# A chunked recurrence fused with a multiplicative FFN on one core: one cumulative sum instead of two from the ninth unit on, and the last output tile stored in two halves

## The chip, the core and the metric

The kernel runs on one core of one Trainium2 chip. The time is device microseconds of one launch. Lower is better.

A core has a tensor engine (PE, with its weight loads shown apart as PEld), a vector engine (DVE), a scalar engine (ACT), a general engine (POOL) and a sync engine (SP) that here only issues DMAs. Each engine works through its own queue in the order in which the program lists its instructions.

## The reference, cut to what matters

Attention: four batches, eight heads, 768 tokens, head size 48. The state of a head decays by `w` per channel and takes in an outer product per token:

```
for t in range(S):
    cur = einsum('bhd,bhe->bhde', u * k[t], v[t])
    y[:, :, t] = einsum('bhd,bhde->bhe', r[t], state + cur)
    state = w[t][..., None] * state + einsum('bhd,bhe->bhde', k[t], v[t])
```

Its result, 3072 tokens by 384 channels, goes through an FFN: `a = x @ w1`, `b = x @ w2` (384 to 1024), `h = a * b @ w3` (1024 to 1024), `out = h @ w_out` (1024 to 384). All inputs and the output are float32.

## The kernel before, in words

**Units.** The tokens are cut into 24 units of 128 tokens (4 batches of 6 units, all eight heads together: a tile of 128 partitions by 384). The step-by-step recurrence becomes matrix work per unit (`att(n)`): with the running sum of log w, k is multiplied by exp(-sum) and r by exp(sum), and a masked product of the two gives what a token takes from earlier tokens of its unit. A state per head pair carries the rest from unit to unit. The steps of a unit `n`, with the engine that does each:

- `ld_w`, `ld_k`, `ld_r`, `ld_v`: four loads of 192 KB each, issued by SP. k and r share a tile `kr_in`; there are eight of each input tile.
- `ln` (ACT): `lw` = log w, in bfloat16.
- `cs0`, `cs1` (PE): two matmuls of 384 columns, with constant triangular matrices `LTn_incl` (minus the sum up to and with the token) and `LT_strict` (the sum up to the token before). Each takes one of five PSUM banks (tiles `g`) which the attention steps share.
- `ex0`, `ex1` (ACT): exp in place in those banks.
- `krt0`, `krt1` (DVE): k and r times the two exponentials, to bfloat16 (`krt`). `krt1` needs `ex1` and the load of r.
- `tr` (PE, eight transposes) and `trs` (the copy out of PSUM) for units 0 to 12; from unit 13 on (`kr_dma`) one DMA transpose issued by SP takes the place of both.
- `vb` (v to bfloat16), `kv` (PE: the unit's contribution to the state, and the unit's whole decay), `pc` (ACT: exp of that decay), `ts`, `st` (DVE: the state), `sb` (its bfloat16 copy).
- `m` (PE: k by r, two banks), `mb0`, `mb1` (DVE: the mask), `y` (PE), `yb` (DVE), `yt` (PE transposes) and `xt` (copy): the FFN's input `xT`.
- `uk1`, `uk2` (POOL: u·k·r, in two multiplications, on tile `uk`), `ds` (DVE: a sum per head) and `yd` (POOL): the token's own term. `uk2` is the last step that reads r as loaded, beside `krt1`.

**FFN.** Nine blocks of 1, 2, 3, 3, ... units. For a block `j`, eight pairs `a`, `b` (three matmuls each), a copy of `a` (`as`, ACT) and a product (`ab`, DVE); then for each of its units `o` (eight matmuls of 384 columns), a copy out of PSUM (`os`) and a store (`st`). The products w3 @ w_out are made once (`wt`, `wtc`, `wm`, `wc`: tiles w3T, wm, w) as soon as those weights are there, so that the FFN needs no h. FFN tiles have three PSUM banks of their own.

**Order.** Nothing is reordered at run time. `Plan` (lines 53 to 208) has a list of steps, each with an engine, an assumed length, what it needs, what buffers or banks it takes and frees, and a rank. It goes through time, starts on each engine the step that can start first (rank breaks ties), and so fixes the order of every engine's queue. `TUNE["nudge"]` shifts single ranks; `TUNE["other"]` lists the steps that go to their second engine (for `trs`, `wtc`: the other of ACT and DVE; `xt`, `os`, `wc`: DVE for ACT; `vb`, `sb`: ACT for POOL; `st`: the ACT queue for SP's). `att` (lines 397 to 585) adds the steps of a unit, `ffn_out` (lines 624 to 646) the output steps, and units are added at a set distance ahead of the FFN. The five big weight loads are issued by POOL, each behind a step named in `TUNE["triggers"]`. Early gaps of PE are filled with matmuls on zeros (`busy`) that compute nothing. Since all instructions go through the helper at line 222, the profile shows that line for all of them; groups are told apart by their tiles.

Of the kernel before, what the change touches and what calls it, by code (L numbers as in the profile page):

```python
# [7 lines left out]
F32 = mybir.dt.float32  # L8
# [10 lines left out]
    kr_dma=13,  # L19
    pair=0,  # L20
    ahead=3, fill=48, cold=9,
    other=[
        "trs0", "trs1", "trs2", "sb2", "sb3", "xt3", "vb4", "xt4", "wc4", "vb6", "sb6", "wtc6", "wc7", "sb7", "vb8",
        "sb8", "st1.0", "xt9", "xt12", "st2.2", "xt13", "vb14", "sb14", "os3.0", "st3.0", "os3.1", "st3.1", "xt16",
        "xt17", "vb18", "vb20", "sb20", "xt20", "os5.0", "st5.1", "xt22", "xt23", "os7.0", "st7.1", "os7.2",
        "st7.2", "st8.1", "st8.2"],
    nudge={
        "ld_w0": -2, "ld_r0": -2, "ld_r6": -27, "ld_w8": -9, "ld_k8": -8, "ld_r8": -34, "ld_v8": -8, "ld_k9": 3,
        "ld_v9": 3, "ld_w10": -1, "ld_w13": 8.5, "ld_k13": 13.5, "ld_k14": -5, "ld_v14": 2, "ld_w15": 7, "ld_k15":
        7, "ld_v15": 7, "ld_w16": 12, "ld_k16": 11, "ld_v16": 12, "ld_w18": -2, "ld_k20": 33, "ld_k21": 30,  # L30
        "ld_v21": 43, "ld_w22": 101, "ld_k22": 33, "ld_r22": 849, "ld_v22": 196, "ld_w23": 139, "ld_k23": 514,
        "ld_v23": 535, "vb1": 75, "yd1": 126, "uk12": 78, "ds2": -49, "tr3": -115, "kv3": -196, "sb3": 175, "yt3":
        210, "cs0.4": -191, "krt1.4": -100, "uk14": 58, "wt1": -93, "wt2": 67, "wt3": 71, "ex0.5": 139, "krt0.5":
        -208, "cs1.5": -36, "ex1.5": -60, "krt1.5": -66, "m5": -29, "ds5": 626, "yt5": 229, "wt4": -42, "wm5": -165,
        "cs0.6": -253, "cs1.6": -84, "tr6": -130, "kv6": -205, "sb6": -168, "m6": 104, "y6": -120, "yb6": 211,
        "wt6": 84, "wtc6": 318, "wt7": 46, "ln7": 59, "cs0.7": 66, "kv7": -219, "ts7": 240, "sb7": -317, "uk17":
        149, "yb7": -88, "o0.0": -59, "a1.0": -276, "ex1.8": -234, "vb8": 49, "kv8": -283, "pc8": -151, "st8": -301,
        "mb0.8": -84, "a1.5": 142, "a1.6": -143, "a1.7": 37, "cs1.9": -90, "krt1.9": 31, "tr9": 31, "pc9": -141,
        "st9": 48, "ds9": 131, "yd9": 147, "b2.0": 416, "krt0.10": 110, "cs1.10": -75, "krt1.10": 402, "vb10": -358,
        "m10": -330, "ds10": 198, "y10": -242, "yt10": 176, "cs1.11": -53, "ex1.11": 492, "krt1.11": 48, "tr11": 26,  # L40
        "vb11": 154, "m11": -426, "mb1.11": -113, "ln12": -56, "cs0.12": 23, "krt0.12": 467, "cs1.12": 35, "ex1.12":
        -181, "tr12": -252, "uk112": 111, "yb12": 314, "a3.0": -100, "a3.2": 46, "b3.2": 183, "cs0.13": -426,
        "krt0.13": -254, "cs1.13": -20, "krt1.13": 33, "kv13": -107, "pc13": -221, "mb1.13": 183, "uk113": 242,
        "ds13": 23, "y13": 40, "xt13": 121, "b3.6": 155, "cs0.14": -79, "cs1.14": -104, "ds14": 313, "vb15": 51,
        "ds15": 111, "y15": -97, "a4.2": 87, "krt0.16": 84, "a4.4": 742, "ln17": -366, "cs1.17": 186, "krt1.17":
        288, "uk117": 572, "ds17": 29, "o4.2": 318, "cs0.18": -437, "krt0.18": 374, "ds18": -91, "y18": 72, "yb18":
        87, "yt18": 1247, "b5.1": 166, "a5.2": 446, "ts19": -150, "a5.6": -448, "b5.7": -40, "o5.0": 409, "o5.2":
        107, "krt1.21": 75, "cs1.22": -204, "y22": 132, "cs0.23": -34, "m23": 94, "o6.1": 17, "o6.2": 537, "a7.1":
        83, "a7.4": 106, "o7.0": 192, "a8.0": -392, "o8.2": -59},
# [177 lines left out]
def kernel(  # L227
# [88 lines left out]
    NS = 3  # L316
# [11 lines left out]
    plan.buffers(w_in=NIN, kr_in=NIN, v_in=NIN, lw=NS, krt=NS, v_bf=3, uk=2, ds=2, yd=3,  # L328
# [28 lines left out]
    def bank(step):  # L357
        return banks(step)[0]
# [37 lines left out]
    def att(n):  # L396
        b, c = divmod(n, NC)
        last = c == NC - 1
        kr_dma = n >= TUNE["kr_dma"]
# [5 lines left out]
        def cs(j):  # L405
            t = T["cs", n, j] = bank(f"cs{j}.{n}")
            pe.matmul(t[:, 0:DM], lhsT=(LTn_incl, LT_strict)[j], rhs=T["lw", n][:, :, 0:D], start=True, stop=True)

        def ex(j):
            t = T["cs", n, j][:, 0:DM]  # L410
            act.activation(t, t, Act.Exp)

# [41 lines left out]
        def kv():  # L454
            t = T["kv", n] = bank(f"kv{n}")[:, 0:HP * (D + 1)].rearrange("d (p e) -> d p e", p=HP)
            for p in range(HP):
                for q in range(2):
                    pe.matmul(t[q * DP:(q + 1) * DP, p, 0:D], lhsT=T["krt", n][:, 0, 2 * p + q, :],
                              rhs=T["vb", n][:, 2 * p + q, :], start=True, stop=True)
            for p in range(HP):  # L460
                pe.matmul(t[:, p, D:D + 1],
                          lhsT=T["lw", n][:, 2 * p:2 * p + 2, :].rearrange("t h d -> t (h d)"),
                          rhs=ones_c, start=True, stop=True)

        def pc():
            t = T["kv", n][:, :, D:D + 1]
            act.activation(t, t, Act.Exp)

        def ts():
            t = T["ts", n] = work.tile([C, HP, D], F32, tag="ts", name="ts_")  # L470
            if c == 0:
                dve.tensor_copy(t, T["kv", n][:, :, 0:D])
            else:
                dve.tensor_add(t, T["st", n - 1], T["kv", n][:, :, 0:D])

        def st():
            t = T["st", n] = work.tile([C, HP, D], F32, tag="st", name="st_")
            dve.tensor_mul(t, T["ts", n], T["kv", n][:, :, D:D + 1].to_broadcast([C, HP, D]))
# [65 lines left out]
        A(f"ln{n}", "ACT", 0.5, ln, needs=[f"ld_w{n}"], take=["lw"], free=[f"ld_w{n}"])  # L544
        for i in range(2):
            A(f"cs{i}.{n}", "PE", 0.165, lambda i=i: cs(i), needs=[f"ln{n}"], bank=1, lag=0.2,
              free=[f"ln{n}"] if i else [])
            A(f"ex{i}.{n}", "ACT", 0.46, lambda i=i: ex(i), needs=[f"cs{i}.{n}"])
            A(f"krt{i}.{n}", "DVE", 0.52, lambda i=i: krt(i),
              needs=[f"ex{i}.{n}", f"ld_k{n}", f"ld_r{n}"][:3 if i else 2] + [f"krt0.{n}"] * i, take=["krt"] * (1 - i),  # L550
              free=[f"cs{i}.{n}", f"ld_k{n}"])
        if not kr_dma:
            A(f"tr{n}", "PE", 0.54, tr, needs=[f"krt1.{n}"], bank=1, lag=0.2, free=[f"krt0.{n}"])
            A(f"trs{n}", "ACT", 0.98, trs, needs=[f"tr{n}"], take=["trs"], free=[f"tr{n}"], alt=("DVE", 0.68))
        else:
            A(f"trs{n}", "SP", 1.8, trs, needs=[f"krt1.{n}"], take=["trs"], free=[f"krt0.{n}"], rows=1500, rank=-3)
        A(f"vb{n}", "POOL", 0.52, vb, needs=[f"ld_v{n}"], take=["v_bf"], free=[f"ld_v{n}"], alt=("ACT", 0.49))
        if not last:
            A(f"kv{n}", "PE", 0.36, kv, needs=[f"krt0.{n}", f"vb{n}"], bank=1, lag=0.2, free=[f"krt0.{n}", f"ln{n}"])
            A(f"pc{n}", "ACT", 0.18, pc, needs=[f"kv{n}"])  # L560
            old = [f"st{n - 1}"] if c else []
            A(f"ts{n}", "DVE", 0.32, ts, needs=[f"kv{n}"] + old, take=["ts"], free=old)
            A(f"st{n}", "DVE", 0.32, st, needs=[f"ts{n}", f"pc{n}"], take=["st"], free=[f"ts{n}", f"kv{n}"])
            A(f"sb{n}", "POOL", 0.7, sb, needs=[f"st{n}"], take=["sb"], free=[f"st{n}"], alt=("ACT", 0.5))
        if pair:
            A(f"m{n}", "PE", 0.33, m, needs=[f"trs{n}"], take=["m"], lag=0.2)
            A(f"mb0.{n}", "DVE", 1.19, lambda: mb(0), needs=[f"m{n}"], take=["mbf"], free=[f"m{n}"])
        else:
            A(f"m{n}", "PE", 0.33, m, needs=[f"trs{n}"], bank=2, lag=0.2)
            for q in range(2):  # L570
                A(f"mb{q}.{n}", "DVE", 0.65, lambda q=q: mb(q), needs=[f"m{n}"] + [f"mb0.{n}"] * q,
                  take=["mbf"] * (1 - q), free=[f"m{n}:{q}"])
        A(f"uk1{n}", "POOL", 1.03, uk1, needs=[f"ld_k{n}", "uc"], take=["uk"])
        A(f"uk2{n}", "POOL", 1.03, uk2, needs=[f"uk1{n}", f"ld_r{n}"], free=[f"ld_k{n}"])
        A(f"ds{n}", "DVE", 0.52, ds, needs=[f"uk2{n}"], take=["ds"], free=[f"uk1{n}"])
# [48 lines left out]
    def ffn_out(j, t_):  # L624
# [7 lines left out]

        def os():
            t = T["os", j, t_] = work.tile([P, DM], F32, tag="o_sb", name="o_sb", bufs=3)
            copy_on(f"os{j}.{t_}", t, T["o", j, t_])

        def st():
# [4 lines left out]
          take=["f"], lag=0.2, free=[f"ab{j}.0"] if t_ == hi - lo - 1 else [])  # L642
        A(f"os{j}.{t_}", "ACT", 0.45, os, needs=[f"o{j}.{t_}"], take=["o_sb"], free=[f"o{j}.{t_}"], rank=EV,
# [108 lines left out]
```

## Time and profile before

| | |
|---|---|
| median of 9 runs | 181.47 us (180.4 to 184.51) |
| the profiled execution | 180.4 us |
| its span, first to last instruction | 178.7 us |
| PE, DVE, ACT, POOL busy | 169.6, 138.8, 101.8, 90.0 us |
| granted clock of PE | 0.997 |
| bytes read and written | 27.8 and 4.7 MB |

How to read it: the span is what the trace covers; the 1.7 us beside it are the launch's. "Busy" adds up the time in which an engine had an instruction under way. A matmul's duration in the trace runs from its start to its modelled end, and the next one starts before that; so what a matmul costs a PE with no gaps is the distance from one start to the next. Rows of groups read: engine, operation, out<-in, shape, count, then busy us and mean ns of one, then idle time of the engine before them and who ended it.

### The profile page before, as it was taken

The page shows a single profiled execution, that of the slowest core. Times are in us where ns is not written, and L with a number is a line of the kernel's source. Part 1 is how long each engine was busy: PE and PEld are TensorE (multiplying, and loading weights), DVE is VectorE, ACT ScalarE, POOL GpSimd, SP SyncE. Part 2 cuts the span into 40 slices and gives each one's busy share as a digit, 9 for nine tenths or more (in the row PEclk, how much of TensorE's full clock was granted, in tenths as well). Part 3 has the DMA queues.
Part 4 walks back from the last instruction along what each step waited for, and adds up shares of the span by engine and source line. Part 5 has one row for each costly group of instructions (what it writes and reads, how often), then busy time and mean ns, then how long its engine had stood idle before and what let it go on. Part 6 is the DMA issues. An engine that isn't in the chain of part 4 may idle for free.

```text
span 178.7 us, 4690 instructions
## 1 busy us (share of the span) xinstructions
PE 169.6 (95%) x1738; PEld 106.6 (60%) x1738; DVE 138.8 (78%) x296; ACT 101.8 (57%) x235; POOL 90.0 (50%) x133
## 2 busy tenths in 40 slices
PE   7989878999999999999999999999999999999992
PEld 2445356777676756667665665655656656566560
DVE  7587735735998998998999899898989988864520
ACT  4333137425697799896787485574656753424421
POOL 4399460207288658489851577951569265100000
PEclk9999999999999999999999999999999999999998
DMA  6999999998999999999999999999999998103013
GB/s 117 192 190 212 200 220 191 194 207 169 193 195 178 241 193 207 189 168 220 233 202 177 186 260 182 188 224 161 206 211 165 229 172 189 22 25 111 0 68 108
DMA packets 117832, 31.23 MB, mean 175 GB/s; under 512 B 111921, under 2 KB 116018, under 8 KB 117810
## 3 DMA queue, kind: packets, MB, share of 16 engines
q1 hardware_dynamic: 113616, 24.72, 82.8%
q0 software_dynamic: 2896, 4.46, 13.6%
q10 hardware_dynamic: 1298, 1.77, 3.2%
q8 instruction: 13, 0.21, 0.5%
q14 instruction: 9, 0.07, 0.2%
HBM read 27.79 MB, written 4.72 MB: 182 GB/s over the span
## 4 chain that ended last, share of the span: by engine, by line
PE 78%; ACT 2%; issue 1%; DVE 0%; ACTq 0%
PE g L222 19%; PE a L222 17%; PE b L222 17%; PE o_ps L222 17%; PE wm L222 6%; PE wt L222 2%; ACT o_sb L222 1%; DVE w3T L222 0%; ACT sbd L222 0%; ACT g L222 0%; ACT xT L222 0%; ACT lw L222 0%; ACTq L222 0%; ACT trs L222 0%
## 5 line engine op out<-in xcount | busy, mean ns | idle before, releaser
L222 PEld LDWEIGHTS <-w_bf 128*128 128x128 bf16 x496 | 41.8, 97 | 23.0 <-issue 2.0
L222 ACT COPY a_sb<-a 128x384 f32<-128x384 f32 (+2 forms) x72 | 31.9, 444 | 29.8 <-PE a L222 27.7
L222 DVE TENSOR_TENSOR abT<-a_sb,b 128x384 bf16<-128x384 f32 (+2 forms) x72 | 36.5, 507 | 10.7 <-ACT a_sb L222 5.5
L222 PE MATMUL b<-xT,w_bf 128*128 128x384 bf16 (+2 forms) x216 | 43.1, 308 | 1.2 <-DMA w_bf<-in_moe_w_dram 1.1
L222 PE MATMUL a<-xT,w_bf 128*128 128x384 bf16 (+2 forms) x216 | 43.1, 308 | 0.5 <-ACT xT L222 0.5
L222 PE MATMUL o_ps<-w,abT 128*128 128x384 bf16 x192 | 34.3, 326 | 0.0
L222 DVE TENSOR_TENSOR mbf<-g,mask 128x512 bf16<-128x512 f32 x48 | 31.8, 685 | 1.7 <-PE g L222 1.6
L222 POOL TENSOR_TENSOR uk<-kr_in,u_bc 128x384 f32<-128x384 f32 x24 | 23.9, 997 | 13.0 <-DMA kr_in<-in_k_dram 12.1
L222 ACT ACTIVATE g<-g 128x384 f32<-128x384 f32 (+1 forms) x68 | 24.8, 385 | 8.4 <-PE g L222 6.4
L222 DVE TENSOR_TENSOR krt<-kr_in,g 128x384 bf16<-128x384 f32 x48 | 25.6, 549 | 5.1 <-ACT g L222 3.6
L222 POOL TENSOR_TENSOR uk<-uk,kr_in 128x384 f32<-128x384 f32 x24 | 24.0, 999 | 8.8 <-DMA kr_in<-in_r_dram 7.4
L222 POOL TENSOR_TENSOR yd<-v_bf,ds 128x384 bf16<-128x384 bf16 x24 | 19.8, 829 | 16.0 <-DVE ds L222 11.6
L222 PEld LDWEIGHTS <-abT 128*128 128x128 bf16 x192 | 18.2, 97 | 11.0
L222 ACT ACTIVATE lw<-w_in 128x384 bf16<-128x384 f32 x24 | 12.6, 524 | 7.5 <-DMA w_in<-in_w_dram 5.4
L222 POOL CAST v_bf<-v_in 128x384 bf16<-128x384 f32 x18 | 9.0, 505 | 14.8 <-DMA v_in<-in_v_dram 10.4
L222 ACT COPY o_sb<-o_ps 128x384 f32<-128x384 f32 x19 | 9.1, 479 | 12.0 <-PE o_ps L222 11.6
L222 PEld LDWEIGHTS <-trs 48*128 48x128 bf16 (+1 forms) x272 | 10.7, 95 | 8.6 <-issue 2.5
L222 PEld LDWEIGHTS <-krt 128*64 128x64 bf16 (+1 forms) x264 | 10.6, 105 | 8.0 <-issue 3.2
L222 DVE TENSOR_TENSOR y_bf<-g,yd 128x384 bf16<-128x384 f32 x24 | 13.3, 553 | 1.5 <-PE g L222 0.9
L222 DVE TENSOR_REDUCE ds<-uk 128x8 f32<-128x384 f32 x24 | 13.1, 544 | 0.0
L222 PE MATMUL idle<-busy 128*128 128x512 bf16 (+8 forms) x38 | 10.8, 399 | 1.3 <-DVE busy L222 1.3
L222 PE MATMUL wm<-wo_bf,w3T 128*128 128x384 bf16 x64 | 11.4, 327 | 0.0
(114 smaller groups left out, 188.1 us busy)
## 6 DMA issues: line engine op xcount, KB each, us to landing
w_in<-in_w_dram SPq DMA_DIRECT2D x24, 192.0 KB, 4.6
kr_in<-in_k_dram SPq DMA_DIRECT2D x24, 192.0 KB, 4.5
kr_in<-in_r_dram SPq DMA_DIRECT2D x24, 192.0 KB, 4.5
v_in<-in_v_dram SPq DMA_DIRECT2D x24, 192.0 KB, 4.4
out_dram<-o_sb SPq DMA_DIRECT2D x15, 192.0 KB, 3.4
w_bf<-in_moe_w_dram POOLq DMA_DIRECT2D x2, 1024.0 KB, 13.4
out_dram<-o_sb ACTq DMA_DIRECT2D x9, 192.0 KB, 3.4
w_bf<-in_moe_w_dram POOLq DMA_DIRECT2D x2, 768.0 KB, 9.0
```

What stands on the lines that cost most here:

```text
L222: return self.tc.keep_in_program_order(f(*a, **k))
```

## The change

Two things in the code, and a new list of choices.

From unit 8 on (`one`), there is one cumulative sum. `cs0` alone is computed, as before minus the sum up to and with the token. `ex0` writes exp of it into a second bank; `ex1` writes exp of its negative in place. That second one is one token too far for r, so r is multiplied by exp(-log w): `wi` (ACT) makes that from `lw`, and `rw` (POOL) multiplies it into the loaded r in place, after `uk2` has read it. `krt1` needs `rw` where it needed the load of r. The matmul with `LT_strict` is gone for these 16 units.

The output tile of the last unit is copied out in two halves of 192 columns, the first by ACT and the second by DVE, and each half has its own store, from the ACT queue and from SP's.

`TUNE["other"]` and `TUNE["nudge"]` are new throughout, and three assumed lengths of PE steps in the plan are others (`tr` 0.45 for 0.54, `kv` 0.44 for 0.36, `m` 0.42 for 0.33). A variant `wide` of `kv` and `ts` is written but switched off (99). The triggers, the blocks and `kr_dma` stay.

```diff
+    wide=99,
+    one=8,
     other=[
-        "trs0", "trs1", "trs2", "sb2", "sb3", "xt3", "vb4", "xt4", "wc4", "vb6", "sb6", "wtc6", "wc7", "sb7", "vb8",
-        "sb8", "st1.0", "xt9", "xt12", "st2.2", "xt13", "vb14", "sb14", "os3.0", "st3.0", "os3.1", "st3.1", "xt16",
-        "xt17", "vb18", "vb20", "sb20", "xt20", "os5.0", "st5.1", "xt22", "xt23", "os7.0", "st7.1", "os7.2",
-        "st7.2", "st8.1", "st8.2"],
+        "xt0", "sb2", "sb3", "wtc0", "xt4", "wc1", "wc4", "st0.0", "xt8", "xt9", "os1.1", "sb10", "xt10", "vb11",
+        "st2.0", "st2.2", "vb14", "sb14", "os3.0", "st3.0", "st3.1", "st3.2", "sb15", "sb16", "xt16", "vb17",
+        "os4.1", "st4.1", "st4.2", "vb18", "sb18", "xt19", "vb20", "sb20", "os5.2", "st5.2", "xt23"],
     nudge={
-        "ld_w0": -2, "ld_r0": -2, "ld_r6": -27, "ld_w8": -9, "ld_k8": -8, "ld_r8": -34, "ld_v8": -8, "ld_k9": 3,
...
-        7, "ld_v15": 7, "ld_w16": 12, "ld_k16": 11, "ld_v16": 12, "ld_w18": -2, "ld_k20": 33, "ld_k21": 30,
-        "ld_v21": 43, "ld_w22": 101, "ld_k22": 33, "ld_r22": 849, "ld_v22": 196, "ld_w23": 139, "ld_k23": 514,
-        "ld_v23": 535, "vb1": 75, "yd1": 126, "uk12": 78, "ds2": -49, "tr3": -115, "kv3": -196, "sb3": 175, "yt3":
...
+        "ld_w5": -1, "ld_k7": -1.5, "ld_w10": -2, "ld_v11": -1, "ld_k13": -2, "ld_w15": 2.5, "ld_r15": 1, "ld_w16":
+        -3, "ld_v16": -10, "ld_w19": -2, "ld_w20": -2, "ld_r20": -2, "ld_w22": 49, "ld_k22": 178, "ld_v22": 212,
+        "ld_v23": 534, "mb0.0": -31, "mb1.0": -16, "ds0": -89, "yd0": -119, "krt0.1": -90, "krt1.1": -74, "ts0.1":
...
+        def ex_one(j):
+            if j == 0:
+                T["cs", n, 1] = T["cs", n, 0]
+                T["cs", n, 0] = bank(f"ex0.{n}")
+            act.activation(T["cs", n, j][:, 0:DM], T["cs", n, 1][:, 0:DM], Act.Exp, scale=(1.0, -1.0)[j])
+
+        def wi():
+            t = T["wi", n] = work.tile([C, H, D], F32, tag="wi", name="wi")
+            act.activation(t, T["lw", n][:, :, 0:D], Act.Exp, scale=-1.0)
+
+        def rw():
+            t = T["kr_in", n][:, 1]
+            pool.tensor_mul(t, t, T["wi", n])
...
+        if one:
+            A(f"cs0.{n}", "PE", 0.165, lambda: cs(0), needs=[f"ln{n}"], bank=1, lag=0.2, free=[f"ln{n}"])
+            A(f"ex0.{n}", "ACT", 0.47, lambda: ex_one(0), needs=[f"cs0.{n}"], bank=1)
+            A(f"ex1.{n}", "ACT", 0.47, lambda: ex_one(1), needs=[f"ex0.{n}"])
+            A(f"wi{n}", "ACT", 0.5, wi, needs=[f"ln{n}"], take=["wi"], free=[f"ln{n}"])
         for i in range(2):
-            A(f"cs{i}.{n}", "PE", 0.165, lambda i=i: cs(i), needs=[f"ln{n}"], bank=1, lag=0.2,
-              free=[f"ln{n}"] if i else [])
-            A(f"ex{i}.{n}", "ACT", 0.46, lambda i=i: ex(i), needs=[f"cs{i}.{n}"])
+            if not one:
+                A(f"cs{i}.{n}", "PE", 0.165, lambda i=i: cs(i), needs=[f"ln{n}"], bank=1, lag=0.2,
+                  free=[f"ln{n}"] if i else [])
+                A(f"ex{i}.{n}", "ACT", 0.46, lambda i=i: ex(i), needs=[f"cs{i}.{n}"])
             A(f"krt{i}.{n}", "DVE", 0.52, lambda i=i: krt(i),
-              needs=[f"ex{i}.{n}", f"ld_k{n}", f"ld_r{n}"][:3 if i else 2] + [f"krt0.{n}"] * i, take=["krt"] * (1 - i),
-              free=[f"cs{i}.{n}", f"ld_k{n}"])
+              needs=[f"ex{i}.{n}", f"ld_k{n}", f"rw{n}" if one else f"ld_r{n}"][:3 if i else 2] + [f"krt0.{n}"] * i,
+              take=["krt"] * (1 - i),
+              free=[f"{'ex0' if i == 0 else 'cs0'}.{n}" if one else f"cs{i}.{n}", f"ld_k{n}"])
...
+        if one:
+            A(f"rw{n}", "POOL", 1.0, rw, needs=[f"wi{n}", f"uk2{n}"], free=[f"wi{n}"])
...
+        def os_half(i):
+            t = T["os", j, t_, i] = work.tile([P, DM // 2], F32, tag=f"o_h{i}", name="o_h", bufs=1)
+            copy_on(f"os{j}.{t_}.{i}", t, T["o", j, t_][:, i * DM // 2:(i + 1) * DM // 2])
...
+        if lo + t_ == NU - 1:
+            for i, (e, length, q) in enumerate((("ACT", 0.27, "ACT"), ("DVE", 0.32, "SP"))):
+                A(f"os{j}.{t_}.{i}", e, length, lambda i=i: os_half(i), needs=[f"o{j}.{t_}"], free=[f"o{j}.{t_}"], rank=EV)
+                A(f"st{j}.{t_}.{i}", q, 0.4, lambda i=i: st_half(i), needs=[f"os{j}.{t_}.{i}"], rows=225, rank=-1)
+            return
```

## The prediction, made before the changed kernel was run

> **What bounds the kernel now.** First the page's busy line and its slices.
>
> ```profile
> PE 169.6 (95%) x1738; PEld 106.6 (60%) x1738; DVE 138.8 (78%) x296; ACT 101.8 (57%) x235; POOL 90.0 (50%) x133
> ...
> PE   7989878999999999999999999999999999999992
> ...
> DVE  7587735735998998998999899898989988864520
> ...
> PEclk9999999999999999999999999999999999999998
> DMA  6999999998999999999999999999999998103013
> ```
>
> PE is full from the eighth slice (about 34 us) to the last but one, at full clock. DMA is full too, but only until about 152 us, so PE is the candidate and DMA the next one. Busy time can hide gaps, so I read the timeline of PE for the distance between starts:
>
> ```profile
> 49.18 0.32 PE L222 MATMUL g<-lw,LT_strict 128*128 128x384 bf16 x1
> 49.34 0.32 PE L222 MATMUL g<-lw,LTn_incl 128*128 128x384 bf16 x1
> 49.50 1.05 PE L222 MATMUL wt<-I,w_bf 128*128 128x128 bf16 x16
> ```
>
> A cumulative sum lasts 0.32 us but the next matmul starts 0.16 later: its price is 0.16, not 0.32. The chain of waits has 32 output matmuls of the same width in 5.21 us, 0.163 each, which I use. The window from 34 to 152 us has PE busy for 117.68 of 118.00, and its one gap of note (0.32, at 63.28) waits for a copy of xT; going through the starts up to 175 us shows none hidden. So in 141 us a microsecond taken from PE is a microsecond of the end, if the others keep up. The windows of the tightest stretch tell how near they are:
>
> ```profile
> core 0: us, PE busy (x) PEld busy (x) DVE busy (x) ACT busy (x) POOL busy (x), PEclk, DMA share, GB/s
> 60.00:70.00 10.00, 9.68 (x125) 5.99 (x124) 8.77 (x21) 9.69 (x24) 6.46 (x9) 1.00 1.11 221
> 70.00:80.00 10.00, 10.00 (x111) 6.45 (x110) 9.60 (x22) 8.95 (x23) 6.81 (x12) 1.00 1.20 178
> 80.00:90.00 10.00, 10.00 (x120) 6.57 (x118) 9.48 (x21) 7.19 (x15) 8.29 (x12) 1.00 1.14 226
> ```
>
> DVE has 2.1 us free of 30, ACT 4.2, POOL 8.4.
>
> **The change part by part.** *The cumulative sum.* Units 8 to 23 lose one matmul of 384 columns: 16 x 0.163 = **2.6 us** off PE, all in the full stretch (unit 8's is after 60 us). Its weight load lay beside PE and counts nothing.
>
> *wi* is 16 more activations on ACT. The trace has no exp from SBUF to SBUF; the nearest rows are log w (0.524) and exp in PSUM (0.478). Bounds 0.48 to 0.54, value 0.52: 8.3 us on ACT, which has 57% busy; `wi` needs only `lw`, so it lies beside `cs0`. Only one table load is in the trace (1.28 us at the start) though log and exp alternate; `wi` is an exp, so no load comes with it. `ex0` in two banks instead of one does the same reading and writing (0.478).
>
> *rw* is 16 more multiplications on POOL, f32 by f32 in place. The same form is there:
>
> ```profile
> L222 POOL TENSOR_TENSOR uk<-uk,kr_in 128x384 f32<-128x384 f32 x24 | 24.0, 999 | 8.8 <-DMA kr_in<-in_r_dram 7.4
> L222 ACT ACTIVATE lw<-w_in 128x384 bf16<-128x384 f32 x24 | 12.6, 524 | 7.5 <-DMA w_in<-in_w_dram 5.4
> ```
>
> 16 x 1.0 = 16 us, taking POOL from 90 to about 106 of 176. It costs nothing while attention runs ahead of PE's need. But here the change adds a wait: `krt1` waited for r's landing and now for `uk1`, `uk2` and `rw` in POOL's queue, at least 2 us after r. Behind a waiting `krt1` on DVE stand masks and FFN products (`ab`), behind these PE's FFN banks. Also `cs0`'s bank is held until `krt1`. In the plan's order this is allowed for; if it fails, it is the second rival below.
>
> More work on POOL could also slow DVE; against that, `krt` lasts 543 to 556 ns over all its 48 instances, with POOL busy or not, so I count nothing for it.
>
> *New engines for steps.* Counted from the two lists: three `trs`, two `xt` and one and a half `os` fewer on DVE (3 x 0.688 + 2 x 0.352 + 0.556, less 0.35 for the new half: -3.0 us); on ACT the three `trs` (3 x 1.013), two `xt`, one `sb`, less one `vb`, about +4.5 with the `os`; POOL -0.74 + 0.50. So DVE falls to 136, ACT rises to about 115, none reaches PE. Stores on the ACT queue go from 9 to 10 with the half (0.34 each to issue): hidden.
>
> *The start.* PE is full only from 34 us because weights land late (the first `b` waits 1.06 us for its weights at 23.5). Triggers are unchanged, and the first twenty loads come in the same order in both lists. `vb1` loses its shift of +75 and may go ahead of `uk1` of unit 1, which triggers w2: 0.50 us late at most for that piece. `trs` of units 0 to 2 goes from 0.69 to 1.01, `xt0` from 0.48 to 0.35. Since the order there is new I bound the start by 1.2 us either way (about the one DMA wait seen) and take 0.
>
> *The last tile.* Its rows:
>
> ```profile
> 169.72 5.36 PE L222 MATMUL o_ps<-w,abT 128*128 128x384 bf16 x32
> ...
> 175.12 0.48 ACT L222 COPY o_sb<-o_ps 128x384 f32<-128x384 f32 x1 [0.82 <-PE o_ps L222]
> 175.63 0.34 ACTq L222 DMA_DIRECT2D out_dram<-o_sb  x1
> ```
>
> Half on ACT is 0.32 (between the 0.266 of 128 columns and 0.373 of 256), half on DVE 0.35 (the 192-column copies `ts`). Side by side they end 0.13 sooner. But ACT's timeline has a row against that, `pc` of unit 0:
>
> ```profile
> 9.02 0.16 ACT L222 ACTIVATE g<-g 128x4 f32<-128x4 f32 x1 [0.48 <-DVE ts__209 L222]
> ```
>
> `pc` needs nothing of `ts`; it works on other columns of the same bank and still is held 0.48 us until DVE's `ts` is done. If the halves are held apart in this way too, the second ends at 0.32 + 0.05 + 0.35 = 0.72 for 0.48, 0.24 later. The last store moves half the bytes; whole ones take 1.9 us to land at the end, and halving takes off between 0 and 0.3. Bounds -0.4 to +0.25; I take held apart, and 0 in sum.
>
> The Trainium skill ("PSUM — Partial Sum Buffer", section "PSUM bank collisions raise a hardware error") has it that ACT and DVE must not touch one bank at the same time, reads included; by this rule side by side is out and the halves gain only by the store, by the durations alone they gain 0.13. The difference of 0.37 us is within my range either way.
>
> **Sum.** -2.6 + 0 + 0. The profiled execution took 180.4 (span 178.7), the fastest of the nine runs, so its like becomes 177.8 (span 176.1). The median shown is 181.47, 1.07 above; I give the forecast for a median: 181.47 - 2.6 = **178.9**. 0.5% (0.9 us) is about what a measurement of this kernel tells from no change.
>
> **Rivals.** *One: DMA sets the tail.* The loads end near 149 us whatever PE does, and the last unit's chain runs from there:
>
> ```profile
> 148.94 0.56 DVE L222 TENSOR_TENSOR krt<-kr_in,g 128x384 bf16<-128x384 f32 x1
> ...
> 149.87 1.24 SPq L222 DMA_TRANSPOSE trs<-krt  x1
> ...
> 160.62 0.65 PE L222 MATMUL a<-xT,w_bf 128*128 128x384 bf16 x3
> ```
>
> The last block's FFN starts at 160.62; with PE 2.6 ahead it should start at 158.0. From the issue of the transpose to its first matmul are 2.4 to 4.3 us, and then 0.42 + 1.35 + 0.5 + 0.6 + 0.5 + 0.4 with hops near 0.7: 156.7 to 158.6. Two output tiles (1.3 each) can be put in between. Against it: the new list loads v of unit 23 last, needed later than r, which came last before; but r now has `rw`, 1 us, behind it. If it binds, about half of the gain comes back: 180.2.
>
> *Two, the slower side: `rw` crowds 60 to 90 us.* Six units pass there. POOL 21.55 + 6 x 1.0 = 27.6, and its waits for loads in that stretch (0.96, 0.70, 0.45, 0.53) make 30.2 of 30; DVE gets `xt8`, `xt10`, `os1.1`: 27.85 + 1.26 = 29.1; ACT 25.82 + 3.1 - 1.4 = 27.5. If POOL makes `krt1` late and DVE's queue stands behind it, PE waits, at most the 1.0 of `rw` per unit. It decides from 2.6 / 6 = 0.43 us per unit: there the gain is gone (181.5); at 0.7 per unit it is 181.47 - 2.6 + 4.2 = 183.1. For it: three engines above 90%. Against: POOL is busy only 3.5 of 10 us in 90 to 100 and in 120 to 130, and attention runs ahead of the FFN.
>
> *Three: a better start.* The new order saves up to the 1.2 us above: 177.7.
>
> That the matmuls stay is excluded: the code calls `cs(0)` alone.
>
> **How the numbers follow.** Forecast 178.9: 0.46. Better start: 0.12. Tail by DMA, 180.2: 0.14, nearly all still faster. Crowding: 0.12 that it eats about the gain, 0.16 that it costs more. Faster 0.46 + 0.12 + 0.12 = 0.70, same 0.02 + 0.12 = 0.14, slower 0.16. The range runs from 177.3 (better start and the -0.4 of the tile) to 182.8, which leaves out about a tenth on either side.
>
> **What would show it.** 16 fewer PE matmuls, 8 `LT_strict` left; PE's full stretch still starting near 34 us and ending near 172.5; no new row of PE waiting for DVE or ACT above 1 us; from the last matmul to the end of the span 3.6 us as before. Wrong if PE shows gaps at 60 to 90 us with `krt` waiting for POOL, or before the last block's first matmul, or if the start moves by more than 1.2 us.

## The result and the profile after

| | before | after |
|---|---|---|
| median of all executions | 182.1 us (63; 180.4 to 187.19) | 182.46 us (21; 178.65 to 183.45) |
| ratio to before | | 0.9902, 95% interval 0.986 to 0.9945 |
| the profiled execution | 180.4 us, span 178.7 | 181.66 us, span 180.0 |

This ratio, like every ratio below, leaves out every execution more than 1.5% above the fastest of its kernel, which for the changed kernel keeps only the 5 of 21 up to 181.12 us, so that it speaks for them, while the medians over all executions are alike. The profiled execution has a granted clock of 0.981 over its span; 18 of the 21 have 0.968 to 0.981, and the three fastest have 1.0. It shows what the 18 may share: it starts late.

First the page of the changed kernel: busy time, then slices of 4.5 us each.

```profile
PE 169.1 (94%) x1723; PEld 106.4 (59%) x1723; DVE 135.7 (75%) x291; ACT 111.3 (62%) x258; POOL 105.1 (58%) x148
...
PE   7899189899999999999999999999999999999992
...
DVE  7477055664489899999999999988999997972610
...
PEclk9969969999999999999999999999999999999999
DMA  6999999999899899999989999999999999202013
```

The fifth slice (18 to 22.5 us) is new: PE at 1, DVE at 0, and right after it the clock at 6. Before, PE and DVE had 8 and 7 there. From the ninth slice on PE is full again to the end.

That asks for the time in three pieces rather than as one sum: the start (up to the first `wm` matmul, which ends the wait for the big weights), the stretch from there to the last matmul's end, and the tail from there to the end of the span. From the timelines:

| | first `wm` | end of last matmul | stretch | tail | span |
|---|---|---|---|---|---|
| before | 35.93 | 175.08 | 139.15 | 3.62 | 178.7 |
| after | 40.06 | 176.45 | 136.39 | 3.55 | 180.0 |
| difference | +4.13 | +1.37 | **-2.76** | -0.07 | +1.3 |

The change does what it is for, 2.76 us in the stretch, and in this execution the start takes back 4.13. The windows that were tightest before are as tight as expected, and PE does not wait in them (columns as in the prediction):

```profile
60.00:70.00 10.00, 10.00 (x134) 6.68 (x132) 9.53 (x22) 8.05 (x19) 9.20 (x15) 1.00 0.91 202
70.00:80.00 10.00, 10.00 (x128) 6.69 (x125) 9.64 (x21) 8.95 (x20) 9.62 (x13) 1.00 1.36 197
80.00:90.00 10.00, 10.00 (x118) 6.63 (x117) 9.42 (x22) 8.74 (x20) 9.19 (x13) 1.00 1.05 224
```

POOL is busy for 28.0 of 30 us, PE for 30.00 of 30. The groups of the new and the halved steps:

```profile
L225 POOL TENSOR_TENSOR kr_in<-kr_in,wi 128x384 f32<-128x384 f32 x16 | 16.0, 1000 | 1.9 <-ACT wi L225 1.0
L225 ACT ACTIVATE wi<-lw 128x384 f32<-128x384 bf16 x16 | 8.4, 524 | 0.8 <-POOL sbd L225 0.4
```

Both have the durations that their nearest rows before had.

**Where the start went.** POOL's queue in the changed kernel (a `DMA_DIRECT2D` here is the issue of a weight load):

```profile
9.66 0.93 POOL L225 DMA_DIRECT2D w_bf<-in_moe_w_dram  x1
10.61 1.01 POOL L225 TENSOR_TENSOR uk<-kr_in,u_bc 128x384 f32<-128x384 f32 x1
11.55 0.80 POOL L225 DMA_DIRECT2D w_bf<-in_moe_w_dram  x1
...
22.81 0.99 POOL L225 TENSOR_TENSOR uk<-uk,kr_in 128x384 f32<-128x384 f32 x1 [4.10 <-DMA kr_in<-in_r_dram]
23.75 0.80 POOL L225 DMA_DIRECT2D w_bf<-in_moe_w_dram  x1
```

and before:

```profile
9.94 0.93 POOL L222 DMA_DIRECT2D w_bf<-in_moe_w_dram  x1
...
13.44 0.80 POOL L222 DMA_DIRECT2D w_bf<-in_moe_w_dram  x1
```

The second weight load, w2, is triggered by `uk1` of unit 1. Before, `sb` and `yd` of unit 0 stood ahead of `uk1` in POOL's queue; now `uk1` comes first, so w2 is issued at 11.55 and not at 13.44. r of unit 2 had been issued by SP at 9.87 (before: 9.66). By the start of `krt1`, which waited for it, it landed near 18.15 before, and near 22.77 now: 8.5 and 12.9 us under way. DVE's `krt1` and then PE waited for it. Before:

```profile
9.66 0.99 SPq L222 DMA_DIRECT2D kr_in<-in_r_dram  x1
...
18.15 0.56 DVE L222 TENSOR_TENSOR krt<-kr_in,g 128x384 bf16<-128x384 f32 x1 [0.85 <-DMA kr_in<-in_r_dram]
```

and now:

```profile
9.87 0.99 SPq L225 DMA_DIRECT2D kr_in<-in_r_dram  x1
...
22.77 0.56 DVE L225 TENSOR_TENSOR krt<-kr_in,g 128x384 bf16<-128x384 f32 x1 [4.71 <-DMA kr_in<-in_r_dram]
```

```profile
23.38 0.61 PE L225 MATMUL g<-I,krt 128*128 128x128 bf16 x4 [4.60 <-DVE krt L225]
```

The same wait held `uk2` of unit 2 on POOL, and behind it the issue of the next weight load: 23.75 (before: 19.20). The weights for `wm` land later by that: the first `wt`, which works on them, starts at 34.04 (before: 29.71).

What moved meanwhile is shown by the two DMA queues from 14 to 18 us in the changed kernel (packets, MB, share of the 16 engines); q0 has POOL's weight loads and q1 what SP issued:

```profile
q0 software_dynamic: 373, 0.73, 96.2%
q1 hardware_dynamic: 367, 0.07, 15.6%
```

Before, q0 moved 0.63 MB there and q1 0.20. Both queues together bring about the same, and the weights take the greater part. Whether the order of two loads is the cause is the first thing that the experiments ask.

### The profile page after: what moved, and what is told of

The parts are those of the page before. It is cut to its first block, busy times and chain, and to the rows that moved or that the text cites. A ratio compares the mean times of both kernels' runs of the same rounds, so it can differ in the third digit from the quotient of the medians.

```text
span 180.0 us, 4705 instructions
## 1 busy us (share of the span) xinstructions
PE 169.1 (94%) x1723; PEld 106.4 (59%) x1723; DVE 135.7 (75%) x291; ACT 111.3 (62%) x258; POOL 105.1 (58%) x148
## 4 chain that ended last, share of the span: by engine, by line
PE 79%; DMA 13%; SPq 5%; POOL 1%; issue 0%; DVE 0%; ACT 0%
PE g L225 19%; PE o_ps L225 18%; PE a L225 17%; PE b L225 17%; DMA kr_in<-in_r_dram 7%; PE wm L225 6%; DMA w_bf<-in_moe_w_dram 6%; SPq L225 5%; PE wt L225 2%; POOL uk L225 1%; DVE o_h L225 0%; ACT o_h L225 0%
## 5 line engine op out<-in xcount | busy, mean ns | idle before, releaser
L225 ACT COPY trs<-g 128x1024 bf16<-128x1024 bf16 x13 | 13.2, 1014 | 7.5 <-PE g L225 7.2
L225 POOL TENSOR_TENSOR kr_in<-kr_in,wi 128x384 f32<-128x384 f32 x16 | 16.0, 1000 | 1.9 <-ACT wi L225 1.0
L225 POOL CAST v_bf<-v_in 128x384 bf16<-128x384 f32 x19 | 9.6, 503 | 6.6 <-DMA v_in<-in_v_dram 4.3
L225 PE MATMUL idle<-busy 128*128 128x512 bf16 (+9 forms) x38 | 12.2, 440 | 1.3 <-DVE busy L225 1.3
```

Of the source, the lines that this page charges most:

```text
L225: return self.tc.keep_in_program_order(f(*a, **k))
```

## The experiments

The theory: 2.6 us come off PE, and what is lost is lost at the start, because w2 overtakes r of unit 2. Rivals: the whole new order makes the start (not this one load); the second sum was worth less than 2.6; POOL's new work holds something up; or the loads (DMA) become the bound.

### The start: w2 moved alone

In the changed kernel, w2 goes to another place in the list in which instructions are issued; nothing else is touched.

```diff
+        order.remove("w2")
+        at = order.index("vb1") + 1      # e2: "uk12", the uk1 of unit 2
+        order[at:at] = ["w2"]
```

> The changed kernel with one edit: POOL issues the load of w2 after vb of unit 1 instead of before yd of unit 0, about 2.5 us later (near 14 us for 11.55); nothing else moves. Theory of the start: w2, issued at 11.55, gets in before unit 2's r has landed, r lands at 22.8 for 18.1, PE stands 4.6 us at 18.6 and loses its clock for a while. By it r lands near 18, PE's full stretch starts about 4 us earlier than in the profile of the changed kernel, and the time falls to 177.7 to 179 (before less 2.6). Rival: the late start is PE's own order or a clock that the chip grants, and w2 has no part in it: then 181 to 182.5 as now.

> The changed kernel with w2's load issued still later, after uk1 of unit 2 (near 16 us for 11.55). By the theory of the start r of unit 2 is safe, but w2 itself lands later than in before, where it landed at 23.5 just as the first b wanted it: 1 to 2 us later here, of which PE loses some: 178.5 to 180. Rival (w2 has no part): 181 to 182.5 as the changed kernel now.

Measured, on one chip where the kernel before had a median of 183.22 us: behind `vb1` 180.76 us, ratio 0.9848 (0.9781 to 0.9914); behind `uk12` 180.21 us, ratio 0.9888 (0.9826 to 0.9951). w2 was issued at 13.64 and 16.93. In the first, r of unit 2 landed near 19.0, PE's wait fell from 4.60 to 1.45, and the first `wm` came at 36.72 instead of 40.06; in the second at 37.35, where the first `b` now waited 1.10 for w2 itself. In the first kernel PE's row is:

```profile
19.64 0.40 PE L229 MATMUL g<-I,krt 128*128 128x128 bf16 x4 [1.45 <-DVE krt L229]
```

So one load moved by 2 us gives back 3.3 of the 4.1 us of the start, within the order of the changed kernel. The place further back costs some of it. The medians are above what I expected (177.7 to 179, and 178.5 to 180). The changed kernel was not run beside them, and the intervals of the ratios overlap with its 0.986 to 0.9945: the start is shown by the traces, and what it is worth in the median is not shown here.

The reverse, on the kernel before: `uk11` and w2 put right behind w1.

```diff
+        for n in ["uk11", "w2"]:
+            order.remove(n)
+        at = order.index("w1") + 1
+        order[at:at] = ["uk11", "w2"]
```

> The kernel before with one edit: uk1 of unit 1 and the load of w2 behind it go ahead of sb and yd of unit 0, so that w2 is issued near 11.6 us for 13.44. Theory of the start: r of unit 2 lands 4 us later, PE stands about 4 us near 19 and the time rises by 2 to 4 us, to 183 to 185. Rival (w2 has no part): within 0.5 us of before.

Measured 185.19 us, ratio 1.0118 (1.0064 to 1.0172). w2 was issued at 11.54, r of unit 2 landed near 22.57, the first `wm` came at 39.56 (before: 35.93), and the stretch stayed at 139.16 (139.15). PE's waits in the start:

```profile
14.66 0.34 PE L226 MATMUL g<-I,y_bf 128*128 128x128 bf16 x3 [2.41 <-DVE y_bf L226]
...
23.18 0.40 PE L226 MATMUL g<-I,krt 128*128 128x128 bf16 x4 [2.49 <-DVE krt L226]
```

The old kernel gets the same late start from this move alone. The wait of 2.41 is for `y_bf`, whose `yd` now stands behind the moved steps on POOL; the 2.49 is r, and since PE stood until r was there, r's landing sets the late start and not the wait ahead of it.

### The sum: the second matmul left out of the kernel before

From unit 8 on `cs1` issues no matmul, and `ex1` reads the first sum with scale 0, so that all other work stays; r is then multiplied by 1.

```diff
+            if j == 1 and n >= 8:
+                return
...
-            act.activation(t, t, Act.Exp)
+            act.activation(t, t, Act.Exp, scale=0.0 if j == 1 and n >= 8 else 1.0)
```

> The kernel before, in its own order, with the second cumulative sum left out from unit 8 on: the matmul is not issued and its exponential works on what the bank holds, times zero, so r is multiplied by 1 there and the output is not the reference's. What it measures is the price of the 16 matmuls alone. Theory: PE has no gaps, so 16 x 0.163 = 2.6 us less than before, 0.9855 of it. Rival: DMA or DVE stands behind PE and gives back half or more: above 0.993.

Measured 182.47 us, ratio 0.9925 (0.9868 to 0.9982). The profiled execution (180.4) has a stretch of 137.13, 2.0 below before's 139.15, but it had the late start too, in the order of before, with w2 issued at 13.16:

```profile
22.17 0.40 PE L222 MATMUL g<-I,krt 128*128 128x128 bf16 x4 [4.49 <-DVE krt L222]
```

The expectation (0.9855) was missed: the ratio lies just under the rival's 0.993, and its interval reaches over that. Two things follow. The sixteen matmuls are worth 2.0 in this stretch, for 2.6 expected; it has 0.50 us of PE gaps in it (before: 0.32), so that most of what is missing stays open here. And 13 us is no safe place for w2: the start of this kernel is that of before, and yet r came as late as in the changed kernel. Whether it lands in time is open there from one execution to the next.

### A steady start, and the pieces of the change on it

With w2 behind `uk12` as the base (the first kernel here is the second of the start's pair again, on another chip), the matmul with `LT_strict` is issued beside (its sum is overwritten by the other); then `wi` and `rw` are left out, so that r is multiplied by a wrong factor; and the same move of w2 is made in the kernel before.

```diff
+            if n >= 8:     # e6
+                pe.matmul(t[:, 0:DM], lhsT=LT_strict, rhs=T["lw", n][:, :, 0:D], start=True, stop=True)
...
         def rw():          # e7; wi likewise
-            t = T["kr_in", n][:, 1]
-            pool.tensor_mul(t, t, T["wi", n])
+            pass
```

> The kernel of e2 once more (the changed kernel with w2's load issued after uk1 of unit 2), as the base for e6 and e7 on the same chip. Theory: with r of unit 2 safe its times lie close together, 179.5 to 182, as in e2.

> The base of e5, but in units 8 to 23 the matmul with LT_strict is issued as well, into the same bank ahead of the one that counts; nothing else moves. This puts the 16 removed matmuls back on PE alone. Theory: PE is the bound in the full stretch, so 16 x 0.163 = 2.6 us above e5. Rival (another engine or DMA stands right behind PE in the changed kernel, so that PE has slack): under 1.3 us above e5.

> The base of e5 with wi and rw left out, so r isn't multiplied by exp(-log w) from unit 8 on and the output is not the reference's; krt1 waits for r's landing again. It takes 8.4 us off ACT and 16 us off POOL. Theory: both lie beside PE, so within 0.5 us of e5. Rival (rw crowds 60 to 90 us, krt1 late): 1 us or more below e5.

> The kernel before with w2's load issued after uk1 of unit 2 (near 16.5 us for 13.44). Theory of the start: in the kernel before r of unit 2 is late in many executions too, since 13.44 is only a little after r's last packets; later is safe, so the median falls by 1 to 2 us below before and the spread narrows. Rival: the late start is the changed kernel's alone: then no better than before, or 1 us worse since w2 lands later.

On this chip the kernel before had a median of 184.01 (35 runs, 181.14 to 186.8).

| | median of 12 | ratio | stretch | PE idle 90 to 140 us |
|---|---|---|---|---|
| steady start | 181.73 | 0.9935 (0.9885 to 0.9986) | 139.87 | 2.59 |
| sum issued twice | 181.54 | 0.9942 (0.9903 to 0.998) | 139.39 | 0 |
| without `wi`, `rw` | 181.37 | 0.9924 (0.9887 to 0.9961) | 138.98 | 2.05 |
| before, w2 moved | 181.93 | 0.9946 (0.9909 to 0.9983) | 139.15 | 0 |

My expectation failed: the matmuls issued again cost nothing here, and the first two are alike. So are all four, within their intervals: beside the kernel before with the same start, the change gains 0.2 us here, which can't be told from noise. The two kernels with the heavier PE have no gaps from 90 to 140 us; the two with the lighter PE have about as much gap as they save. PE's rows in the first kernel:

```profile
90.44 0.32 PE L229 MATMUL g<-lw,LTn_incl 128*128 128x384 bf16 x1 [0.60 <-ACT lw L229]
...
122.80 0.40 PE L229 MATMUL g<-trs 48*128 48x128 bf16 x8 [0.72 <-DMA trs<-krt]
...
139.51 0.31 PE L229 MATMUL g<-v_bf,krt 128*64 128x48 bf16 x8 [1.38 <-POOL v_bf L229]
```

and POOL's row that the last one waits for:

```profile
138.95 0.50 POOL L229 CAST v_bf<-v_in 128x384 bf16<-128x384 f32 x1 [1.31 <-DMA v_in<-in_v_dram]
```

Each name in the bracket leads to a transfer: `lw` waited for w, `trs` is a transfer itself, `v_bf` waited for v. The engine named beside PE's wait is only the last hop. Leaving out `wi` and `rw` does not take the gaps away, so POOL's new work is not what is late; the loads are. In that kernel, too, the two long waits lead to loads: `lw` waited 1.05 for w at 114.27, and `v_bf` 2.10 for v at 138.00.

The move of w2 in the kernel before narrows its range (181.14 to 186.8) to 181.13 to 183.95, with a median of 181.93 for 184.01: that fits late starts as the source of its longest executions, though none of those was profiled. By the ratio, without them, the move is worth 0.5%.

### Less to load

If the loads are the bound at 90 to 140 us, fewer bytes must bring the matmuls' worth back. From unit 8 on only four heads of v are loaded, and `vb` copies them twice; nothing else changes. Three kernels: the steady start, the same with the sum issued twice, and the kernel before with w2 moved.

```diff
+            if n >= 8:
+                sp.dma_start(T["v_in", n][:, 0:H // 2], src(v)[:, 0:H // 2])
+                return
...
```

> The base of e5 with half of the load of v from unit 8 on (96 KB for 192; vb reads the four loaded heads twice, so heads 4 to 7 get the v of heads 0 to 3 and the output is not the reference's). Every instruction and its order stay; DMA has 1.5 MB less to bring, some 8 us of it at 195 GB/s. New theory: after a good start PE, 2.6 us lighter, catches up with the loads at 90 to 140 us and waits for them (0.6, 0.7 and 1.4 us in e5), so DMA now bounds as much as PE. By it the gaps go and the time falls by 1 to 3 us against e5, to 179 to 180.5. Rival (the waits come from POOL and ACT being crowded): gaps and time stay as in e5.

> The kernel of e9 (half of v from unit 8 on) with the second cumulative sum issued as well, as in e6. New theory: with the loads out of the way PE alone bounds, and the 16 matmuls cost the whole 2.6 us that e6 didn't show: 2.2 to 2.8 above e9. Rival (the 16 matmuls are worth nothing on PE in this order, whatever DMA does): within 1 us of e9.

> The kernel before with w2 after uk1 of unit 2 (e8) and half of v from unit 8 on; output not the reference's, as in e9. New theory: e9 and e11 are then the changed kernel and the kernel before with the start and the loads both out of the way, and differ by the 2.6 us of the matmuls: e11 2 to 3 us above e9. Rival (the new order costs or brings something of its own in the full stretch): a difference under 1.5 or over 3.5 us.

On this chip before had 182.17 us (23 runs).

| | median | ratio | stretch |
|---|---|---|---|
| half of v | 179.36 | 0.9896 (0.9839 to 0.9952) | 136.39 |
| half of v, sum twice | 181.47 | 1.0012 (0.9972 to 1.0052) | 138.78 |
| half of v, before | 182.13 | 1.0055 (1.0017 to 1.0092) | 139.15 |

The windows from 90 to 140 us, of the steady start and then of half of v:

```profile
90.00:140.00 50.00, 47.41 (x499) 29.15 (x499) 45.00 (x95) 37.82 (x94) 34.95 (x44) 1.00 1.13 194
```

```profile
90.00:140.00 50.00, 50.00 (x528) 30.74 (x526) 47.12 (x101) 39.40 (x98) 37.00 (x47) 1.00 1.07 188
```

PE's busy time (the second number) goes from 47.41 to 50.00. With the loads out of the way the sixteen matmuls are worth 2.1 us in the medians (181.47 - 179.36) and 2.39 in the stretch, and the whole change 2.8 (182.13 - 179.36) and 2.76. The stretch of 136.39 is the very one that the changed kernel had in its profiled execution: it fits that the late start gave the loads 4 us of lead there, and that PE did not catch up with them. What loading less is worth in time is not shown: the steady start with all of v was not run on this chip but for the kernel of the next part.

### The last tile in two banks

The steady start (all of v loaded), with the last output tile made as two accumulations of 192 columns, each in a bank of its own, and both copied by ACT.

```diff
+        def o_half(i):
+            t = T["o", j, t_, i] = ps_f.tile([P, DM // 2], F32, tag="f", name="o_ph")
+            for fi in range(FI):
+                pe.matmul(t, lhsT=T["abT", j][:, fi, t_ * P:(t_ + 1) * P], rhs=w34[:, fi, i * DM // 2:(i + 1) * DM // 2],
+                          start=(fi == 0), stop=(fi == FI - 1))
...
```

> The base of e5 with the last output tile computed in two halves of 192 columns in two banks, eight matmuls each, so that ACT copies the first half out while PE makes the second. Output as the reference's. Theory: in one bank DVE's half waits for ACT's (it starts 0.35 us after), in two banks the last copy starts at the last matmul's end and takes 0.32: from the last matmul to the end of the span 3.2 us for 3.54 in the changed kernel; the median within 0.7 us of e5, 0.3 better if it can be seen. Rival (the halves wait for the store and not the bank): 3.5 as before.

Measured 179.09 us, ratio 0.9894 (0.9846 to 0.9943), tail 3.20. The tail of the changed kernel:

```profile
176.48 0.32 ACT L225 COPY o_h<-o_ps 128x192 f32<-128x192 f32 x1 [0.82 <-PE o_ps L225]
...
176.83 0.36 DVE L225 COPY o_h<-o_ps 128x192 f32<-128x192 f32 x1 [4.93 <-ACT o_h L225]
```

and with two banks:

```profile
174.88 0.32 ACT L229 COPY o_h<-o_ph 128x192 f32<-128x192 f32 x1 [0.18 <-PE o_ph L229]
...
175.61 0.32 ACT L229 COPY o_h<-o_ph 128x192 f32<-128x192 f32 x1 [0.41 <-PE o_ph L229]
```

In one bank, DVE begins when ACT has ended, 0.35 us after ACT began, though it reads other columns; its row names ACT's copy as what released it. (The new kernel also has two tiles where there was one and ACT for both copies, so that the bank is not separated from these.) In two banks the first half is copied under the second one's matmuls, and only one copy of 0.32 is left after the last matmul. This kernel computes all of the reference. On its chip it beats the kernel before (182.17); the changed kernel (182.46 over all its executions) and the steady start were not run beside it, so that the expected median (within 0.7 us of the steady start) is not tested.

It kept 1.63 us of PE gaps from 90 to 140 us (stretch 138.42), where half of v had none, and yet its median is no higher (179.09 and 179.36, six runs each). This stands against the loads as a steady loss: in the profiled executions the loads make the gaps, but how often they do, and on which chip, the medians do not tell. Their two starts in the profile (37.08 and 37.86) and the tails (3.20 and 3.45) make 1.0 of the 2.0 that the stretches differ by; the profiled execution was also the slowest of its six (180.39). The rest stays open.

## Why the prediction was right, and where it was not

- **The sum** had the right price. 16 x 0.163 = 2.6 foretold, 2.76 in the stretch of the profiled execution, 2.39 for the matmuls alone on half of v. That 2.76 is above 2.6 is chance: 0.3 of it is a PE gap (0.32 from the first `wm` to 90 us before, 0.01 after) that the new order does not have and the sum did not count. Distance from start to start was the right price; the 0.32 of the row would have foretold twice as much. What went with it, "a microsecond taken from PE is a microsecond of the end, if the others keep up", did not hold everywhere: on the steady start the sixteen matmuls cost nothing in the median (181.54 and 181.73), and the loads did not keep up in the traces.
- **`wi`, `rw` beside PE at nothing** was right: 524 and 1000 ns as taken from the nearest rows, busy sums of 135.7 (foretold 136) and 105.1 (106) on DVE and POOL, and no gain clear of noise without the two. ACT has 111.3 for 115: its rows do add up to 12.9 us more than before (foretold 12.8), but where rows overlap, busy time counts them once. The "one and a half `os` fewer" on DVE is half of one, as the sum in the brackets there has it (five whole copies before, four and a half after).
- **The start failed.** The step read "bound the start by 1.2 us either way (about the one DMA wait seen) and take 0"; it was 4.13 in the profiled execution. It had the place, `uk1` of unit 1 against its neighbours on POOL, and the sign of the move the wrong way about: w2 came 1.9 us earlier, not 0.50 later. The real error is what it took for the cost of a moved issue: only the shift of the load itself. An earlier load is not a gain by itself: here r of unit 2 was 4.4 us longer under way beside it, while q0 moved 0.73 MB and q1 0.07. "Triggers are unchanged, and the first twenty loads come in the same order in both lists" holds for each queue by itself, and not between SP's loads and POOL's. By its own test (wrong "if the start moves by more than 1.2 us") this part is refuted, and the profiled execution took 181.66 where its like was put at 177.8. The two differ by 3.9: 4.13 - 0.16 (the stretch) - 0.07 (the tail).
- **Forecast and result.** 178.9 is 0.986 of 181.47, at the edge of the interval of the ratio, and only the three fastest executions are near it; the median over all is 182.46, close to the range's upper end of 182.8, which a rival had put there that did not occur. So it is partly luck that the forecast came out: an unforeseen loss of 4 us at the start is in the profiled execution and, by their clocks, may be in most of the 21, and the ratio near the forecast comes from the five that are left.
- **Rival one** (DMA as the bound) had the right resource and the wrong place. It looked for it behind the last load; it shows at 90 to 140 us, when the start is good: 1.2 to 2.6 us of gaps in four of the five profiled kernels with all of v, the lighter PE, and a first `wm` near 37 (1.21, 2.59, 2.05, 1.63); the fifth, the first run of the steady start, had 0.16. Its lower bound for the last unit (2.4 us from the issue of the transpose to its first matmul) took the matmul of the unit before; its own came at 154.17, 4.3 after the issue.
- **Rival two** (`rw` crowds 60 to 90 us) fell. Its sum for POOL was near (28.0 of 30 with the work; 27.6 foretold), and PE lost nothing.
- **Rival three** (a better start) did not occur.
- **The last tile** was right: held apart in one bank, 0.36 for DVE's half, tail 3.62 to 3.55, in sum nothing.

## What to carry to other kernels

Split the span into start, full stretch and tail before comparing two versions, and give each its own sum: here -2.8 and +4.1 hide in +1.3, and medians over executions that start differently hide it too. When a change reorders a queue that issues transfers, write down the issue time of every big transfer beside the small ones in flight from the other queues; the small one that the critical path needs first should be landed before the big one is issued. Where PE is lightened, look for the next bound in the same stretch at once: follow each new wait through its hops to the transfer, and test it by loading less.

## What the runs showed of the hardware that was not expected

- A load of 192 KB (r of unit 2) took 8.5 us when the second 768 KB weight load was issued 3.8 us after it, and 12.9 us when that came 1.7 us after it. It is no fixed threshold: with 13.16 instead of 13.44 for w2, in another execution, its `krt1` was late enough for PE to wait 4.49. Over all fourteen profiled executions, `krt1` of unit 2 starts at 22.57 and 22.77 with w2 issued near 11.5 (two), at 18.15, 19.03 and 21.55 with w2 at 13.16 to 13.64 (three), and between 17.84 and 19.47 with w2 at 15.3 or later (nine).
- From 14 to 18 us in the changed kernel, the two queues moved packets one for one (373 and 367), but those of the weights have 2.0 KB and those of SP's loads 0.19 KB on average, so that the bytes went ten to one. Whether larger packets would keep r on time was not tried.
- After PE's wait of 4.60 us in the changed kernel the granted clock was 0.75 and 0.50 in the windows 22 to 24 and 24 to 26 us, and the four transposes that PE did first took 0.61 us, for 0.40 before: the wait costs more than itself. How long PE waits does not decide it alone. In the starts of the profiled executions the clock fell to 0.50, for some 3.4 us each time, after waits of 4.60, 4.49, 2.41, 2.05, 1.60 and 1.45, and did not fall after others of 2.50, 2.49, 2.42 and 2.31. The changed kernel and the one with the sum issued twice have a drop from 8 to 14 us (0.84, 0.50 and 0.81 in the first) without any wait over 0.5 us before it but the first one, 1.25 us at the very start; its cause stays open.
- One such fall takes 0.5 x 3.4 of some 180 us off the mean granted clock, about 0.0094: an execution with one shows 0.990, one with two 0.981, as the profiled one of the changed kernel does. By this estimate, which takes all falls to be of that length, 18 of its 21 executions had at least two of them.
